# Output tiles of 128 x 2 x 512 in two buffers, and stores of 2 KB runs, in a retention and feed-forward kernel

## The chip, the cores and the metric

The kernel runs on one core of a Trainium2 chip. The metric is the device time of one execution in microseconds; the time of a kernel is the median of its runs.

## The reference

Eight batches, eight heads, 576 tokens, 64 dimensions a head: a causal retention (scores times a decay, no softmax), then a feed-forward layer with a hard swish over 4608 tokens, 512 to 2048 to 512 features. All inputs and the output are float32.

```python
scores = scale * np.matmul(q, k.transpose(0, 1, 3, 2))
ret = scores * Dmat[None, :, :, :]          # gamma ** (i - j), zero above the diagonal
x = np.matmul(ret, v) laid out as (B * S, H * D)
h = x @ w_in
g = h * np.clip(h + 3.0, 0.0, 6.0) / 6.0
out = g @ w_out
```

## The kernel before

The tokens of a batch are cut into four chunks of 128 and a tail of 64; two tails of neighbouring batches share a chunk, so there are 36 chunks. The feed-forward part works on blocks of 512 tokens: blocks 0 to 7 are the first 512 tokens of each batch, block 8 gathers the tails. Blocks are finished in the order 0, 1, 2, 3, 4, 5, 6, 8, 7.

The order of all work is written out by hand in `PROGRAM`, one word per step; each engine runs its own instructions in that order, and so does the queue of SP, which issues every load and every store. `l` loads a chunk (q, k, v, 256 KB each, in runs of 256 B), `c` casts one of the three with the decay (mostly on POOL), `x` has ACT issue a DMA transpose of q and k, `s` makes the scores on PE and masks them on DVE (tile `at`), `o` makes the retention output and the running state on PE; ACT copies the output into `xt` (L339) and, but for the last chunk of a batch, the state into `s16` (L345). The `xp` and `state` banks in PSUM have one buffer each, so the `o` of a chunk needs ACT's copies of the chunk before. `u` and `h` are the up projection: PE into a PSUM bank `ph`, then ACT (`u`, L371) and DVE (`g`, L376).

The down projection of block 0 is plain: four PSUM banks `po`, one of 128 tokens each, copied out in turn by ACT and DVE (`down_plain_end`) and stored one by one (L414). Of every other block it is a product by quadrants in the manner of Strassen: `e` builds sums of quarters of `g` on DVE (tiles `ss`), and the word `P<block>.<n>` runs one of seven products, in the order P1, P5, P6, P2, P7, P4, P3. A block of the output has four quadrants of 256 tokens by 256 features. P2 ends quadrant (0, 0), which ACT copies out (L519); P7, P4 and P3 end (1, 1), (1, 0) and (0, 1), which DVE adds up out of `accC` or `accD` and `Z` or `W` (L522, L525, L528). The four accumulators A, C, B, D and the `ph` banks share four PSUM buffers under the tag `mm`.

Each quadrant gets a tile `osb` of 128 x 2 x 256 float32 (two groups of 128 tokens), of which there are four buffers, and a store of its own right behind the word that fills it: 256 KB in runs of 1 KB (L532). For block 8 a quadrant leaves in four stores of 64 tokens, 64 KB each (`store`, L418). In `PROGRAM` other words stand between the products; block 1's stretch reads

```
P1.0 P1.1 x11 P1.2 P1.3 e1.3.0.8 s9 o8 x12 e1.4.0.8 l18 P1.4 o9 c13.0g
c13.2g c13.1g l19 s10 P1.5 P1.6 x13
```

and block 2's and 3's ends

```
P2.3 s16 c19.2g o15 c20.0g c20.1g e2.4.0.8 P2.4 s17 o16 x19 P2.5 l24 c20.2g l25 P2.6
P3.3 c23.2g s21 c24.1g o20 P3.4 l29 x23 c24.2g c25.0v c25.1g P3.5 P3.6 l30
```

where `.3` is P2, `.4` P7, `.5` P4 and `.6` P3. A tile of a tag with n buffers can be filled only when the readers of an earlier tile of that buffer are done; for `osb` that is the landing of its stores.

Of the kernel before, what the change touches and what calls it, by code (L numbers as in the profile page):

```python
# [10 lines left out]
FP32 = mybir.dt.float32  # L11
FP16 = mybir.dt.float16
ACTF = mybir.ActivationFunctionType
ALU = mybir.AluOpType
# [69 lines left out]
def kernel(  # L84
# [9 lines left out]
    nc = tc.nc  # L94
    B, H, S, D = q.shape
    NTOK, DM = out.shape
    DFF = moe_w_in.shape[1]
    P = 128
# [4 lines left out]
    NFC = DFF // P  # L103
    NCC = DM // P
    BLK = 512
    COL_UP, COL_DOWN = (5, 6, 8, 7), (4, 5, 6, 8, 7)
    gamma = [1.0 - 2.0 ** (-5.0 - h) for h in range(H)]
    lng = [float(np.log(g)) for g in gamma]
# [2 lines left out]
    work = ctx.enter_context(tc.tile_pool(name="work", bufs=2))  # L111
# [14 lines left out]
    tmat = [const.tile([P, NFC // 2, 256], FP16, name=f"tmat{i}") for i in range(4)]  # L126
    xtail = const.tile([P, NCC, BLK], FP16)
    ident = const.tile([P, P], FP16)
    zero16 = const.tile([P, BLK], FP16)
    NS16 = 2  # L130
# [170 lines left out]
    def ret2(c):  # L301
# [24 lines left out]
        if kind == 0:  # L326
            if t == 0:
                state[0] = psum.tile([P, HP, D], FP32, tag="st", name="state")
                xts[b] = work.tile([P, NCC, BLK], FP16, tag="xt", bufs=3,
                                   name="xt")  # L330
# [25 lines left out]
    def g_new(kb):  # L356
        gs[kb] = work.tile([P, NFC, BLK], FP16, tag="g", bufs=2, name="g")

    def mul(ps, lhs, rhs, start, stop, halves=True):

        if not halves:
            nc.tensor.matmul(ps, lhs, rhs, start=start, stop=stop,  # L362
                             skip_group_check=True)
            return
        for z in range(2):
            nc.tensor.matmul(ps[z * D:z * D + D], lhs[:, z * D:z * D + D], rhs,  # L366
                             start=start, stop=stop, skip_group_check=True)

    def hswish(ph, dst):
        u = work.tile([P, BLK], FP32, tag="u", bufs=3, name="u")  # L370
        nc.scalar.activation(u, ph, ACTF.Relu, bias=0.5,  # L371
                             scale=1.0 / 6.0)
        sh = list(dst.shape)
        uv = u if len(sh) == 2 else u.rearrange("p (a i) -> p a i", a=sh[1])
        pv = ph if len(sh) == 2 else ph.rearrange("p (a i) -> p a i", a=sh[1])
        nc.vector.scalar_tensor_tensor(out=dst, in0=uv, scalar=1.0,  # L376
                                       in1=pv, op0=ALU.min, op1=ALU.mult)

    def up(kb, fc, nwarm=0):
# [3 lines left out]
        xt = xts[kb] if kb < B else xtail  # L383
        ph = psum.tile([P, BLK], FP32, tag="mm", bufs=4, name="ph")
        if nwarm:
# [24 lines left out]
    def store(kb, i0, osb_ap, n0, nn):  # L410

        if kb < B:
            base = kb * S + i0
            nc.sync.dma_start(out[base:base + P, n0:n0 + nn], osb_ap)  # L414
        else:
            for z in range(2):
                base = (i0 // TAIL + z) * S + MAIN
                nc.sync.dma_start(out[base:base + TAIL, n0:n0 + nn],  # L418
                                  osb_ap[z * TAIL:(z + 1) * TAIL, :])
# [12 lines left out]

    def down_plain_end(kb, pos):
        for mc, po in enumerate(pos):
            ob = work.tile([P, DM], FP32, tag="osb", bufs=4, name="osb")
            if mc % 2:
                nc.vector.tensor_copy(ob, po)
            else:
                nc.scalar.copy(ob, po)
            store(kb, mc * P, ob, 0, DM)  # L440


    HF = NFC // 2
# [24 lines left out]
    def wq(i, j):  # L468
        return wout16[:, i * HF:(i + 1) * HF, j * 256:(j + 1) * 256]

    def product(kb, name):
        g = gs[kb]
        d = dn.setdefault(kb, {})

        def gq(i, j):
            return lambda fc, m: g[:, j * HF + fc,
                                   i * 256 + m * P:i * 256 + m * P + P]

        def sq(w):
            t_ = ssum[(kb, w)]  # L480
            return lambda fc, m: t_[:, fc, m * P:m * P + P]

        acc, first, last, lhs, rhs = {
            "P1": ("A", True, False, gq(0, 0), wq(0, 0)),
            "P2": ("A", False, True, gq(0, 1), wq(1, 0)),
            "P6": ("B", True, False, None, tmat[1]),
            "P7": ("B", False, False, None, tmat[2]),
            "P4": ("D", True, True, gq(1, 1), tmat[3]),
            "P5": ("C", True, False, None, tmat[0]),
            "P3": ("C", False, True, None, wq(1, 1)),  # L490
        }[name]
        if lhs is None:
            lhs = sq({"P6": 2, "P7": 3, "P5": 1, "P3": 4}[name])
        if first:
            d[acc] = psum.tile([P, 2, 256], FP32, tag="mm", bufs=4,
                               name="acc" + acc)
        ps = d[acc]
        for fc in range(HF):
            for m in range(2):
                mul(ps[:, m, :], lhs(fc, m), rhs[:, fc, :],  # L500
                    first and fc == 0 and m == 0, fc == HF - 1 and m == 1,
                    kb in COL_DOWN)
        if name == "P1":
            d["X"] = work.tile([P, 2, 256], FP32, tag="X", bufs=1, name="X1")
            nc.scalar.copy(d["X"], ps)
        elif name == "P6":
            d["W"] = work.tile([P, 2, 256], FP32, tag="W", bufs=1, name="W1")
            nc.vector.tensor_tensor(out=d["W"], in0=ps, in1=d["X"], op=ALU.add)
        elif name == "P5":
            return  # L510
        else:
            if name == "P7":
                d["Z"] = work.tile([P, 2, 256], FP32, tag="Z", bufs=1, name="Z1")
                nc.vector.tensor_tensor(out=d["Z"], in0=ps, in1=d["X"],
                                        op=ALU.add)
                ps = d["C"]
            ob = work.tile([P, 2, 256], FP32, tag="osb", bufs=4, name="osb")
            if name == "P2":
                nc.scalar.copy(ob, ps)  # L519
                i, j = 0, 0  # L520
            elif name == "P7":
                nc.vector.tensor_tensor(out=ob, in0=ps, in1=d["Z"], op=ALU.add)  # L522
                i, j = 1, 1
            elif name == "P4":
                nc.vector.tensor_tensor(out=ob, in0=ps, in1=d["Z"], op=ALU.add)  # L525
                i, j = 1, 0
            else:
                nc.vector.tensor_tensor(out=ob, in0=ps, in1=d["W"], op=ALU.add)  # L528
                i, j = 0, 1
            if kb < B:  # L530
                base = kb * S + i * 256
                nc.sync.dma_start(  # L532
                    out[base:base + 256, j * 256:(j + 1) * 256]
                    .rearrange("(m p) n -> p m n", p=P), ob)
            else:
                for m in range(2):
                    store(kb, i * 256 + m * P, ob[:, m, :], j * 256, 256)


    wst = {}  # L540
# [65 lines left out]
    for z in range(2):  # L606
        nc.gpsimd.iota(pos[z * TAIL:(z + 1) * TAIL, 4:5], pattern=[[0, 1]],
                       base=MAIN, channel_multiplier=1,
# [4 lines left out]
    for h in range(H):  # L613
        nc.vector.memset(lngt[:, h:h + 1], lng[h])
    nc.vector.tensor_tensor(out=etab, in1=etab, op=ALU.subtract,
                            in0=pos.unsqueeze(2).to_broadcast([P, 9, H]))
    nc.vector.tensor_tensor(out=etab, in0=etab, op=ALU.mult,
                            in1=lngt.unsqueeze(1).to_broadcast([P, 9, H]))
# [25 lines left out]
    def act(w):  # L644
# [16 lines left out]
        elif kind == "c":  # L661
            cast(order[n[0]], n[1], ENG[e])
        elif kind == "x":
            xpose(order[n[0]])
        elif kind == "y":
            xpose_pe(order[n[0]], "xp", e)
        elif kind in "sS":
            ret1(order[n[0]], *n[1:], two=(kind == "S"))
        elif kind == "o":
            ret2(order[n[0]])  # L670
        elif kind == "W":
            wload(*n)
        elif kind == "w":
            wcast(*n, e)
        elif kind == "t":
            tbuild(n[0])
        elif kind == "e":
            enc(*n)
        elif kind == "u":
            up(*n)  # L680
        elif kind == "h":
            up_half(n[0], n[1], n[2:4], *n[4:])
        elif kind == "p":
            if n[0] == 0:
                plain.extend(down_plain_begin(0))
            down_plain_part(0, plain, 2 * n[0], 2 * n[0] + 2)
            if n[0] == HF - 1:
                down_plain_end(0, plain)
        else:
            product(n[0], PROD[n[1]])  # L690
# [31 lines left out]
```

## Time and profile before

| what | value |
|---|---|
| median of 5 runs | 305.24 us (303.3 to 307.98) |
| the profiled execution | 303.3 us, its span 301.1 us |
| busy, ACT / DVE / POOL | 145.3 / 238.9 / 104.7 us |
| queue 1 (SP's loads and stores) | 120128 packets, 46.15 MB |
| queue 10 (ACT's transposes) | 29568 packets, 7.34 MB |
| stores at L532 | 28, 256 KB, 372 to 1873 ns on SP |
| stores at L418 (block 8) | 16, 64 KB, 540 to 1146 ns on SP |
| stores at L414 (block 0) | 4, 256 KB, in runs of 2 KB |
| first and last copy at L519 | 80.3 and 291.6 us |
| mean granted TensorE clock | 0.993 |

The span goes from the first to the last instruction. An engine's busy time leaves out its queue's issuing and waiting. A line of a timeline gives the start, the duration, the engine, the line of the kernel, the operation, and what it writes and reads; in square brackets stand the idle time before it and what ended that. "SPq" and "ACTq" are the engines' instruction queues, where DMAs are issued. The landing of a DMA is when its last completion has come.

### The profile page before, as it was taken

Reading aid. Unit: us, or ns where it says so; the run is one execution under the profiler, and the core shown is the slowest. Engines: PE = TensorE matmul, PEld = TensorE weight load, DVE = VectorE, ACT = ScalarE, POOL = GpSimd, SP = SyncE. Lnnn points to the kernel's source line nnn. Section 1 sums busy time; section 2 is a strip of 40 time slices with the busy share of each in tenths; the row PEclk is TensorE's granted clock in tenths of the full one; section 3 lists DMA queues with packets and bytes.
Section 4 is the critical chain, followed back from the end, with each engine's and each line's share of the span. In section 5 each row is a group of like instructions: output and inputs, shape, how many; then the busy total and the mean of one; then the engine's idle time right before and its main releaser. Section 6 shows DMA issues by size and latency. Waiting matters only on the chain.

```text
span 301.1 us, 8762 instructions
## 1 busy us (share of the span) xinstructions
PE 290.1 (96%) x3695; PEld 209.6 (70%) x3695; DVE 238.9 (79%) x341; ACT 145.3 (48%) x267; POOL 104.7 (35%) x116
## 2 busy tenths in 40 slices
PE   8889998998999999999999999999999999999994
PEld 3565354787788878547854796579657975895693
DVE  6757744989978999798778997998699768857953
ACT  2778704864237723475157424753476136306610
POOL 5354644866248636454942122334200000000000
PEclk9979999999999999999999999999999999999999
DMA  7999999999999999999999998998522130014003
GB/s 246 306 359 386 223 290 205 222 208 211 268 157 188 247 241 215 190 196 251 244 193 266 236 201 174 244 243 128 131 20 53 39 107 0 3 47 97 0 27 117
DMA packets 149735, 54.05 MB, mean 179 GB/s; under 512 B 134848, under 2 KB 145088, under 8 KB 149696
## 3 DMA queue, kind: packets, MB, share of 16 engines
q1 hardware_dynamic: 120128, 46.15, 70.2%
q10 hardware_dynamic: 29568, 7.34, 19.1%
q8 instruction: 29, 0.48, 0.7%
q14 instruction: 10, 0.08, 0.1%
HBM read 36.70 MB, written 9.44 MB: 153 GB/s over the span
## 4 chain that ended last, share of the span: by engine, by line
PE 86%; DVE 5%; ACT 3%; DMA 2%; POOL 2%; issue 1%; POOLq 0%; ACTq 0%
PE ph L362 19%; PE ph L366 18%; PE accB L366 6%; PE accC L366 6%; PE accA L366 6%; PE po L362 5%; PE accB L362 4%; PE xp L309 3%; PE sc L284 3%; PE accD L366 3%; DMA st<-in_q_dram 2%; PE accA L362 2%; PE accC L362 2%; PE xp L254 2%; DVE ss L464 2%; DVE g L376 2%
## 5 line engine op out<-in xcount | busy, mean ns | idle before, releaser
L371 ACT ACTIVATE u<-ph 128x512 f32<-128x512 f32 x144 | 84.5, 597 | 63.4 <-PE ph L362 26.9
L376 DVE SCALAR_TENSOR_TENSOR g<-u,ph 128x512 f16<-128x512 f32 x144 | 94.7, 683 | 23.2 <-ACT u L371 22.1
L362 PE MATMUL ph<-xt,win 128*128 128x256 f16 (+1 forms) x464 | 72.5, 314 | 0.0
L362 PEld LDWEIGHTS <-win 128*128 128x128 f16 x464 | 44.4, 98 | 23.2
L177 POOL TENSOR_TENSOR qk<-st,tq 128x512 f16<-128x512 f32 x29 | 32.1, 1107 | 49.7 <-PE state L334 15.6
L366 PEld LDWEIGHTS <-win 128*64 128x64 f16 x512 | 28.7, 110 | 24.4
L177 POOL TENSOR_TENSOR v<-st,tkv 128x512 f16<-128x512 f32 x29 | 32.5, 1125 | 35.7 <-DMA st<-in_v_dram 17.5
L295 DVE TENSOR_TENSOR at<-sc,mask 128x1024 f16<-128x1024 f32 (+1 forms) x34 | 39.0, 1155 | 5.8 <-PE sc L284 5.7
L366 PE MATMUL ph<-xt,win 128*64 128x512 f16 x384 | 42.8, 379 | 0.0
L366 PEld LDWEIGHTS <-ss 128*64 128x64 f16 x640 | 34.5, 110 | 0.5 <-DVE ss L464 0.3
L177 POOL TENSOR_TENSOR qk<-st,tkv 128x512 f16<-128x512 f32 x26 | 29.0, 1114 | 8.5 <-DMA st<-in_k_dram 8.4
L339 ACT ACTIVATE xt<-xp 128x512 f16<-128x512 f32 x32 | 19.1, 597 | 19.6 <-PE xp L315 17.1
L362 PEld LDWEIGHTS <-g 128*128 128x128 f16 x208 | 19.6, 98 | 10.4 <-issue 2.0
L366 PEld LDWEIGHTS <-g 128*64 128x64 f16 x480 | 26.1, 110 | 0.6
L464 DVE TENSOR_TENSOR ss<-g 128x1024 f16<-128x1024 f16 (+1 forms) x30 | 23.5, 793 | 0.3
L309 PE MATMUL xp<-at,v 128*64 128x128 f16 x288 | 20.5, 228 | 1.0 <-ACT xt L339 0.8
L362 PEld LDWEIGHTS <-ss 128*128 128x128 f16 x192 | 18.3, 98 | 3.2 <-DVE ss L464 0.9
L366 PE MATMUL accB<-tmat,ss 128*64 128x256 f16 x320 | 19.2, 273 | 0.0
L366 PE MATMUL accA<-wout,g 128*64 128x256 f16 x320 | 19.1, 273 | 0.0
L309 PEld LDWEIGHTS <-v 128*64 128x64 f16 x288 | 14.7, 111 | 6.1 <-issue 3.1
L519 ACT COPY osb<-accA 128x512 f32<-128x512 f32 x8 | 4.7, 585 | 28.1 <-PE accA L366 17.2
L345 ACT CAST s<-state 64x256 f16<-64x256 f32 x48 | 17.3, 361 | 0.5
(94 smaller groups left out, 319.1 us busy)
## 6 DMA issues: line engine op xcount, KB each, us to landing
st<-in_v_dram SPq DMA_DIRECT2D x32, 256.0 KB, 6.2
out_dram<-osb SPq DMA_DIRECT2D x32, 256.0 KB, 4.8
st<-in_q_dram SPq DMA_DIRECT2D x28, 256.0 KB, 5.7
st<-in_k_dram SPq DMA_DIRECT2D x28, 256.0 KB, 5.8
wst<-in_moe_w_in_dram SPq DMA_DIRECT2D x4, 512.0 KB, 7.4
tmat<-in_moe_w_in_dram SPq DMA_DIRECT2D x4, 512.0 KB, 8.2
wst<-in_moe_w_out_dram SPq DMA_DIRECT2D x4, 512.0 KB, 10.8
g<-in_moe_w_out_dram SPq DMA_DIRECT2D x4, 512.0 KB, 6.3
```

Of the source, the lines that this page charges most:

```text
L177: eng.tensor_tensor(out=dst, in0=st[:, ix, :, :], in1=tab.unsqueeze(2).to_broadcast([P, H, D]), op=ALU.mult)
L254: nc.tensor.matmul(ps, zero16[:, 0:P], zero16[:, 0:w], start=True, stop=True)
L284: nc.tensor.matmul(sc[z][:, p, :], qt[z * D:z * D + D, HP + p, :], qt[z * D:z * D + D, p, :], start=True, stop=True)
L295: nc.vector.tensor_tensor(out=dst, in0=src, op=ALU.mult, in1=m[:, :].unsqueeze(1).to_broadcast([P, n, P]))
L309: nc.tensor.matmul(xp[rows[z], p, :], vt[:, 2 * p + z, :], at[:, z, p, :], start=(p == 0), stop=False, skip_group_check=True)
L339: nc.scalar.activation(xts[b][:, :, t * P:(t + 1) * P], xp, ACTF.Copy, scale=0.125)
L345: nc.scalar.copy(s16[rows[z], :, rows[z]], sp[rows[z], :, :])
L362: nc.tensor.matmul(ps, lhs, rhs, start=start, stop=stop, skip_group_check=True)
L366: nc.tensor.matmul(ps[z * D:z * D + D], lhs[:, z * D:z * D + D], rhs, start=start, stop=stop, skip_group_check=True)
L371: nc.scalar.activation(u, ph, ACTF.Relu, bias=0.5, scale=1.0 / 6.0)
L376: nc.vector.scalar_tensor_tensor(out=dst, in0=uv, scalar=1.0, in1=pv, op0=ALU.min, op1=ALU.mult)
L464: nc.vector.tensor_tensor(out=dst, in0=a, in1=c, op=op)
```

## The change

The tile `osb` becomes 128 x 2 x 512 float32, twice as large, with two buffers in place of four: one tile for the upper 256 tokens of a block (quadrants (0, 0) and (0, 1)), one for the lower (1, 0) and (1, 1). The four output operations of a block write halves of these tiles. Except for block 7, which is done last, nothing is stored behind P2 and P7; behind P4 the whole lower tile is stored, and behind P3 the whole upper one, 512 KB each in runs of 2 KB. Block 7 stores each quadrant as before, out of the wider tile. Block 8 leaves in eight stores of 64 tokens x 512 features, four behind P4 and four behind P3. In block 0 the four 128-token results go in pairs into two tiles; their four stores stay as they are. `PROGRAM` is not touched.

```diff
+    LAST_BLK = 7
...
     def down_plain_end(kb, pos):
         for mc, po in enumerate(pos):
-            ob = work.tile([P, DM], FP32, tag="osb", bufs=4, name="osb")
-            if mc % 2:
-                nc.vector.tensor_copy(ob, po)
+            if mc % 2 == 0:
+                ob = work.tile([P, 2, DM], FP32, tag="osb", bufs=2, name="osb")
+                nc.scalar.copy(ob[:, 0, :], po)
             else:
-                nc.scalar.copy(ob, po)
-            store(kb, mc * P, ob, 0, DM)
+                nc.vector.tensor_copy(ob[:, 1, :], po)
+            store(kb, mc * P, ob[:, mc % 2, :], 0, DM)
...
-            ob = work.tile([P, 2, 256], FP32, tag="osb", bufs=4, name="osb")
+            i, j = {"P2": (0, 0), "P7": (1, 1), "P4": (1, 0), "P3": (0, 1)}[name]
+            if ("o", i) not in d:
+                d["o", i] = work.tile([P, 2, DM], FP32, tag="osb", bufs=2,
+                                      name="osb")
+            ob = d["o", i][:, :, j * 256:(j + 1) * 256]
             if name == "P2":
                 nc.scalar.copy(ob, ps)
-                i, j = 0, 0
...
             else:
-                nc.vector.tensor_tensor(out=ob, in0=ps, in1=d["W"], op=ALU.add)
-                i, j = 0, 1
+                nc.vector.tensor_tensor(
+                    out=ob, in0=ps, in1=d["W" if name == "P3" else "Z"],
+                    op=ALU.add)
+            if kb == LAST_BLK:
+                js = slice(j * 256, (j + 1) * 256)
+            elif name in ("P4", "P3"):
+                js = slice(0, DM)
+            else:
+                return
+            ob = d["o", i][:, :, js]
             if kb < B:
                 base = kb * S + i * 256
                 nc.sync.dma_start(
-                    out[base:base + 256, j * 256:(j + 1) * 256]
+                    out[base:base + 256, js]
                     .rearrange("(m p) n -> p m n", p=P), ob)
             else:
                 for m in range(2):
-                    store(kb, i * 256 + m * P, ob[:, m, :], j * 256, 256)
+                    store(kb, i * 256 + m * P, ob[:, m, :], 0, DM)
```

More of the change, by code (lines that the diff above doesn't have):

```diff
@@ L516, in product @@
                 ps = d["C"]
-            ob = work.tile([P, 2, 256], FP32, tag="osb", bufs=4, name="osb")
+            i, j = {"P2": (0, 0), "P7": (1, 1), "P4": (1, 0), "P3": (0, 1)}[name]
[3 more added lines that the diff above has]
+            ob = d["o", i][:, :, j * 256:(j + 1) * 256]
             if name == "P2":
                 nc.scalar.copy(ob, ps)
-                i, j = 0, 0
[L521 to L526, printed above, removed]
-            else:
-                nc.vector.tensor_tensor(out=ob, in0=ps, in1=d["W"], op=ALU.add)
-                i, j = 0, 1
+            else:
+                nc.vector.tensor_tensor(
[8 more added lines that the diff above has]
+            ob = d["o", i][:, :, js]
             if kb < B:
```

## The prediction

> **What bounds the kernel now.** First the page: who is busy, and when.
>
> ```profile
> PE 290.1 (96%) x3695; PEld 209.6 (70%) x3695; DVE 238.9 (79%) x341; ACT 145.3 (48%) x267; POOL 104.7 (35%) x116
> ...
> PE   8889998998999999999999999999999999999994
> ...
> DMA  7999999999999999999999998998522130014003
> ```
>
> PE is busy for 290.1 of 301.1 us, and the DMA engines are full until about slice 28 (210 us): the loads and stores of that stretch stand in a long queue. Next the chain of waits in order of time, around the first stores of the product blocks.
>
> ```profile
> 93.27 7.24 DMA st<-in_q_dram
> ...
> 103.92 0.61 ACT u L371
> 104.55 1.89 DVE g L376 x3
> 106.47 1.08 DVE ss L464
> 107.57 1.96 DVE ss L464
> 109.53 0.05 issue
> 109.58 1.92 PE accB L362 x16
> ```
>
> Up to 109.58 us the chain crosses a load and other engines; from there to 296.79 it stays on PE, without a pause worth naming. So whatever holds PE after 109.58 lengthens the run one for one, and little can be gained there: the list of PE's waits from 99 to 290 us has one entry, 0.2 us. Then SP's queue in order of time:
>
> ```profile
> 97.06 1.79 SPq L157 DMA_DIRECT2D st<-in_v_dram  x1
> 99.33 0.81 SPq L532 DMA_DIRECT2D out_dram<-osb  x1
> ...
> 104.74 0.90 SPq L532 DMA_DIRECT2D out_dram<-osb  x1
> 107.80 0.37 SPq L157 DMA_DIRECT2D st<-in_q_dram  x1
> ...
> 110.77 1.76 SPq L532 DMA_DIRECT2D out_dram<-osb  x2
> ```
>
> These are block 1's stores. Their tiles were written at 80.3 to 88.2 us, but the stores leave at 99.33, 104.74, 110.77 and 112.11: SP runs some 20 us behind the engines. Its last two, looked at alone:
>
> ```profile
> L532 SPq DMA_DIRECT2D out_dram<-osb x2: 416/831/1246, 110.8 to 112.1; - x2
> ...
> DMA to landing us min/median/max: 5.3/5.7/6.0
> ```
>
> They land at 110.77 + 6.0 = 116.8 and 112.11 + 5.3 = 117.4. Last, ACT and PE in block 2, whose P2 is the next to want an output tile:
>
> ```profile
> 114.40 0.58 ACT L519 COPY osb<-accA 128x512 f32<-128x512 f32 x1 [1.34 <-PE accA L362]
> 115.22 0.60 ACT L339 ACTIVATE xt<-xp 128x512 f16<-128x512 f32 x1 [0.23 <-PE xp L315]
> 115.71 0.74 ACT L345 CAST s<-state 64x256 f16<-64x256 f32 x2
> ```
>
> ```profile
> 117.41 0.25 PE L309 MATMUL xp<-at,v 128*64 128x128 f16 x2
> 117.49 0.22 PE L315 MATMUL xp<-qkT,s 128*64 128x128 f16 x2
> ```
>
> **The change, part by part.** *Fewer, wider stores.* Six blocks go from four 256 KB stores to two of 512 KB, block 8 from sixteen of 64 KB to eight of 128 KB, block 7 keeps its four: 20 issues fewer. The bytes are the same. Between 99 and 113 us the two last of block 1 land 0.6 us apart, 256 KB in 0.6 us, some 400 GB/s, and no slice in which stores run alone shows more than 389; block 0's stores, which have runs of 2 KB already, landed no closer (0.8 us). So I price the longer runs at nothing, ends 0 and 0.2 us per 512 KB. An issue on SP costs 0.37 us unobstructed (block 6); two per block is 0.75 us of SP's time, which lies beneath the DMA queue's 5 to 6 us of backlog. If that cover were gone, loads would come 0.75 us earlier, and from 109.58 on PE does not wait for loads.
>
> The Trainium skill, "DMA: Bandwidth & Descriptors", section "Anatomy of one DMA — SWDGE (gpsimd) path", gives each DMA a fixed 2.0 us for its own path, which would by estimate favour merging by 2.0 us per store on a path; here stores left by SP land 0.6 us apart, so the fixed part overlaps. The same page's "Rules for kernel authors" speaks against this change: issue a DMA early and wait for it late. The sum below needs neither.
>
> *When the stores leave.* P2's and P7's stores go; P4's carries the lower rows, P3's the upper. In SP's order block 1's three loads between P2 and P7, and three between P7 and P4, move ahead of two stores. Those loads gain one or two issues (0.8 to 1.7 us); nothing on PE waits for it. Block 2's go likewise: its last store still leaves behind two more chunk loads.
>
> *Two buffers in place of four.* The bytes of SBUF are the same, but the tile that P2 of a block fills is P2's and P3's of the block before, if buffers are taken in turn, and its store is now the **last** of that block. Before, P2 took the buffer whose store left first (99.33, landed 104.9; the copy came at 114.40, so 9.5 us to spare). The prices, block by block:
>
> Block 1 after block 0: the first two plain stores land at 78.1 and 78.9, P2's copy comes at 80.25; the other two at 81.1 and 81.8, P7's write at 83.9. Nothing, with 1.4 us as cover.
>
> Block 2 after block 1: as many bytes stand ahead of the last landing as before, so it stays at 117.4, and ACT's copy waits from 114.40 till then. Behind it on ACT stand the xt copy and the two s casts, 0.58 + 0.60 + 0.74 less 0.1 of overlap: 1.8 us. PE's next retention chunk needs both; it gets them at 117.4 + 1.8 = 119.2 in place of 117.49. **Price 1.7 us**, straight onto PE. Ends: SP sat for 2.1 us ahead of the load at 107.80, waiting for a transpose whose place in the order can shift when DMAs go; without it the landing is 115.3 and the price below nothing, so 0. Such a wait can also fall on the store itself; the longest that one of the stores shows is 2.7 us (block 0's fourth), which makes 4.4. I take the row as it stands.
>
> Block 3 after block 2: that last store leaves at 145.09 and takes 5.9, landing at 151.0; the copy comes at
>
> ```profile
> 145.77 0.59 ACT L519 COPY osb<-accA 128x512 f32<-128x512 f32 x1 [4.66 <-PE accA L362]
> 146.67 0.60 ACT L339 ACTIVATE xt<-xp 128x512 f16<-128x512 f32 x1 [0.32 <-PE xp L315]
> ...
> 153.00 0.60 ACT L371 ACTIVATE u<-ph 128x512 f32<-128x512 f32 x1 [5.73 <-PE ph L362]
> ```
>
> ACT stalls 5.2 us, 3.5 after the first delay. But ACT was going to idle 5.73 us before its next u, and PE meanwhile has P7, P4 and P3 (3 x 1.75 us) until it wants accA's PSUM bank at 151.94, now 153.6; the copy ends at 151.6. The transpose behind it leaves 5 us later for a chunk that PE takes at 164. Nothing, with 2 us as cover; ends 0 and 1.5, if the store lands 3.5 later.
>
> Block 4 after block 3: landed at 167.05 + 4.6 = 171.7, copy at 177.03: nothing. Blocks 5 to 8 and 7: SP has caught up by 207 us, stores land in 2 to 5 us, a block lies 26 us or more from the next: nothing.
>
> *Strided tile halves and the end.* A store or an engine now touches half of a tile while the other half is in use. ACT's xt copy at 58.06 and PE's ph matmul at 58.41 on other columns of the same xt tile overlapped in time, so halves do not wait for each other. The writes keep their 128x512 shape: 0.58 and 0.69 us. Block 7 stores as before, its end is unchanged.
>
> Sum: 1.7 us. The profiled execution took 303.3 with a span of 301.1 us (2.2 around it), so 305.0, span 302.8. It was the fastest of the five runs; on their median of 305.24 the forecast is 306.9, +0.6%.
>
> **Rivals.** *No stall* (25%): SP's 2.1 us wait goes, or the wider stores land sooner, and block 1's last landing falls before 115.7, the point from which PE is not delayed. For it: the wait is a transpose's, not the data's. Against it: the queue is backlogged either way. 305.2, not slower; 304.8 with the 0.2 us and the gaps on PE filled.
> *A later landing* (18%): a wait for a transpose lands ahead of the store, or block 3's cover breaks as well: 2.6 to 4.4 us, 307.8 to 309.6. For it: six such waits stand on SP, 8.8 us in all, and a stalled ACT issues its transposes later.
> *The other buffer* (10%): P2 takes the buffer freed first. Its copy then waits for 116.1 or so (0.4 us), and in block 3 P7's write, at 149.37 before, waits for 151.0; P3's matmuls need accC read by it and start at 151.7, not 150.19, less the shift: 1.1. Together 1.5: 306.7.
> *Faster* (5%): earlier loads shorten the chain. It crosses a load only at 93.27, before the first store that moves. 303.5.
> *The change not as told*: seven blocks' 1024 data packets of 1 KB must be halved, so queue 1 must show at least 3584 packets fewer than 120128, or it did something else.
>
> **How the numbers follow.** The forecast (0.8 to 2.6 us, 306.0 to 307.8) gets 42%. Half a per cent, about what a measurement can tell from no change, is 1.5 us. Slower: two thirds of the forecast (28%), the later landing (18%), 4% of the other buffer: 50%. Same: 14 + 21 + 6 = 41%. Faster: 5 + 4 of no stall: 9%. The range runs from 304.6, no stall with little noise, to 309.4.
>
> **What would show it.** The stores of whole blocks down from 28 to 16 issues and the tail block's from 16 to 8; in block 2 ACT's osb copy ended by a DMA out_dram<-osb, some 3 us long, and an idle PE of 1 to 2 us before L309 or L315; in block 3 a stall of 3 to 5 us on ACT with PE unmoved. PE idle anywhere else, or no wait at either copy, would make the steps wrong.

## The result, and the profile after

| kernel | median | runs | ratio to before, 95% |
|---|---|---|---|
| before | 305.13 us (302.12 to 308.06) | 85 | |
| changed | 306.58 us (303.52 to 309.97) | 43 | 1.005 [1.0033, 1.0066] |

The change costs about 1.5 us: half a per cent. That is just at what a measurement can tell from no change, but the interval lies above 1, so it isn't zero. (Ratios leave disturbed runs out, so they can differ a little from the quotient of two medians.) The profiled execution of the changed kernel took 305.75 us, its span 304.0.

The page's lines on busy time, on SP's queue and on the stores of whole blocks (count, size, median us from issue to landing):

```profile
PE 289.5 (95%) x3695; PEld 208.8 (69%) x3695; DVE 240.3 (79%) x341; ACT 145.3 (48%) x267; POOL 103.9 (34%) x116
...
q1 hardware_dynamic: 116224, 46.15, 70.2%
...
out_dram<-osb SPq DMA_DIRECT2D x12, 512.0 KB, 5.9
```

The change does what it says: the same 46.15 MB in 3904 packets fewer, twelve stores of 512 KB (and four of 256 KB in block 7), at the same work of PE. SP's queue in order of time, around the stores of blocks 1 and 2:

```profile
109.25 1.06 SPq L158 DMA_DIRECT2D st<-in_v_dram  x1
110.42 2.53 SPq L538 DMA_DIRECT2D out_dram<-osb  x2
113.04 0.85 SPq L158 DMA_DIRECT2D st<-in_q_dram  x1
...
135.46 0.57 SPq L538 DMA_DIRECT2D out_dram<-osb  x1
...
144.82 1.68 SPq L158 DMA_DIRECT2D st<-in_v_dram  x1
146.61 1.19 SPq L538 DMA_DIRECT2D out_dram<-osb  x1
```

Block 1's stores now leave together, at 110.42 and 112.55 (the second start is from the single records of the pair), and land at 117.04 and 119.81. Block 2's second store leaves 11 us behind its first, at 146.61, since six loads stand between the two words, and lands at 152.23. Who waits for these landings is told by ACT and DVE in order of time:

```profile
117.10 0.58 ACT L524 COPY osb<-accA 128x512 f32<-128x512 f32 x1 [1.91 <-DMA out_dram<-osb]
117.58 0.60 ACT L340 ACTIVATE xt<-xp 128x512 f16<-128x512 f32 x1
118.07 0.75 ACT L346 CAST s<-state 64x256 f16<-64x256 f32 x2
```

```profile
150.77 0.69 DVE L515 TENSOR_TENSOR Z<-accB,X 128x512 f32<-128x512 f32 x1 [0.55 <-PE accB L363]
152.32 0.69 DVE L526 TENSOR_TENSOR osb<-accC,Z 128x512 f32<-128x512 f32 x1 [0.85 <-DMA out_dram<-osb]
```

```profile
150.57 1.91 PE L363 MATMUL accD<-tmat,g 128*128 128x256 f16 x16
153.07 1.91 PE L363 MATMUL accC<-wout,ss 128*128 128x256 f16 x16 [0.58 <-DVE osb L526]
```

In block 2 P2's copy starts right after the **first** landing of block 1 (117.04), not the last; in `a0` below it does the same, 0.07 us behind a first landing at 118.56. Of the 1.91 us that ACT idled, 1.25 are there without any wait for a store too (`d1` below, where PE ends them), so the store's own share is 0.66 us. ACT is done with the casts at 118.82, and PE comes for them at 119.54: no wait. In block 3 it is not P2's copy but **P7's write** that waits, for the landing at 152.23, and through it PE, because P3's matmuls go into the bank that this write reads. PE's list of waits from 99 to 300 us has this one entry:

```profile
PE accC L363 <- DVE osb L526: 0.6, 1, 0.6
```

Before, no wait stands at either step, on DVE or on PE:

```profile
149.37 0.69 DVE L522 TENSOR_TENSOR osb<-accC,Z 128x512 f32<-128x512 f32 x1
...
150.19 1.91 PE L362 MATMUL accC<-wout,ss 128*128 128x256 f16 x16
```

So the two buffers are not taken in turn: what these waits show is that the next tile gets the buffer that is released first. In a block the upper tile is begun first but stored last. Block 2's upper tile sits where block 1's lower one was, and block 3's lower tile, filled by P7, gets the buffer that block 2's late store holds.

### The profile page after: what moved, and what is told of

Read it like the earlier page. It is cut to its first block, busy times and chain, and to the rows that moved or that the text cites. A ratio compares the mean times of both kernels' runs of the same rounds, so it can differ in the third digit from the quotient of the medians.

```text
span 304.0 us, 8719 instructions
## 1 busy us (share of the span) xinstructions
PE 289.5 (95%) x3695; PEld 208.8 (69%) x3695; DVE 240.3 (79%) x341; ACT 145.3 (48%) x267; POOL 103.9 (34%) x116
## 3 DMA queue, kind: packets, MB, share of 16 engines
q1 hardware_dynamic: 116224, 46.15, 70.2%
## 4 chain that ended last, share of the span: by engine, by line
PE 64%; DMA 15%; SPq 9%; DVE 4%; POOL 4%; issue 1%; ACT 1%; POOLq 0%; ACTq 0%; DVEq 0%
PE ph L367 18%; PE ph L363 12%; PE accB L367 6%; PE accA L367 6%; DMA st<-in_v_dram 5%; PE accC L367 5%; PE po L363 4%; SPq L561 4%; SPq L158 4%; DMA tmat<-in_moe_w_in_dram 3%; DMA out_dram<-osb 3%; PE accD L367 2%; PE xp L310 2%; PE sc L285 2%; DMA qkT<-qk 2%; DMA st<-in_k_dram 2%
## 5 line engine op out<-in xcount | busy, mean ns | idle before, releaser
L178 POOL TENSOR_TENSOR qk<-st,tq 128x512 f16<-128x512 f32 x29 | 30.9, 1066 | 52.7 <-DMA st<-in_q_dram 18.2
L178 POOL TENSOR_TENSOR v<-st,tkv 128x512 f16<-128x512 f32 x29 | 33.7, 1165 | 36.7 <-DMA st<-in_v_dram 10.0
```

The source lines that it names most:

```text
L178: eng.tensor_tensor(out=dst, in0=st[:, ix, :, :], in1=tab.unsqueeze(2).to_broadcast([P, H, D]), op=ALU.mult)
```

## The experiments

One length of the trace separates the kernels better than the whole time: from PE's first matmul of the product ahead of block 2's P2, into `accB` (109.58 us before), to the first matmul of P3 in block 3 (150.19 before). In these traces it holds the only waits that the two buffers made on PE. In the table: when PE gets to the first of the two, the length between them, the length from there to PE's last matmul, and the timed ratio. All lengths are differences of start times in the trace.

| kernel | reaches block 2 | to block 3's P3 | to the last matmul | timed ratio |
|---|---|---|---|---|
| before | 109.6 | 40.61 | 146.28 | |
| `b0` before, again | 111.8 | 40.60 | 146.28 | 1.0035 [1.0001, 1.0068] |
| `b1` before, third | 110.0 | 40.60 | 146.28 | one run |
| `d0` before, fourth | 112.0 | 40.61 | 146.82 | 1.0012 [0.9981, 1.0044] |
| changed | 111.7 | 41.35 | 146.28 | 1.005 [1.0033, 1.0066] |
| `a0` changed, again | 113.4 | 41.14 | 147.77 | 1.0076 [1.0039, 1.0112] |
| `d1` changed, third | 112.7 | 40.94 | 146.28 | 1.0103 [1.0064, 1.0143] |
| `d3` one buffer per half | 112.9 | 40.94 | 146.27 | 1.0058 [1.0027, 1.009] |
| `a1` three buffers | 112.1 | 40.61 | 147.08 | 1.0046 [1.0013, 1.008] |
| `a2` store ahead of loads | 111.1 | 40.61 | 146.89 | 1.0014 [0.9983, 1.0045] |
| `c3` both of these | 111.4 | 40.61 | 146.83 | 1.0006 [0.9972, 1.004] |
| `d2` both, again | 112.4 | 40.61 | 146.28 | 1.0013 [0.9978, 1.0049] |
| `c1` wide tiles, old stores | 113.0 | 40.60 | 146.28 | 1.0022 [0.9988, 1.0056] |
| `a3` store behind a third load | 112.4 | 47.38 | 149.32 | 1.0269 [1.0222, 1.0315] |

**Equal kernels.** No edit: the changed kernel twice more, the one before three times more, to see how far one execution stands for its kernel.

> The changed kernel once more, unedited, for a second profile. Theory 'buffer': its loss is one stall, in block 3, where P7's write on DVE waits for block 2's last store and PE's P3 waits for that write (0.6 us in the first profile); it shows here again, 0.3 to 2.5 us, ratio 1.003 to 1.007. Theory 'early': the 2.1 us that the first profile was late before 105 us, ahead of any store that moved, belong to the change too; then this profile is again about 2 us late there. Rival 'spread': the early 2.1 us are one execution's luck and come out anywhere from -1.5 to +2 us.

> The changed kernel, unedited, on the same chip as its cure: 'buffer' theory 1.004 to 1.009, and P7's write in block 3 again waits for a store; PE's stall there 0.3 to 2 us.

> The kernel before, unedited, for a second profile of it. In the five profiles of the changed kernel and its variants PE begins block 1's first product at 74.1 to 75.4 us, against 72.8 in the one profile of before, and block 0's fourth store leaves at 80.7 to 82.9, against 78.3. Rival 'spread': that one profile was a lucky execution; this one shows 74 to 75.5 and about 81. Theory 'early': the change makes it, and this one shows 72.3 to 73.3 and about 78. Ratio 0.998 to 1.002 either way.

> The same once more, a third profile: 'spread' 73.5 to 75.5 us for block 1's first product, 'early' 72.3 to 73.3.

> The kernel before, submitted like the others, for a second look at what no change at all measures here (1.0035 the first time). 'Chance': 0.998 to 1.002. 'Place' (a submitted kernel reads a little slower than the runs that it is set against): 1.002 to 1.005 again, and the others are to be read from there.

The loss repeats: 307.22 and 306.86 us beside 304.97 and 304.89 for the kernel before in the same groups. So does the noise: against itself the kernel before came out at 1.0035, more than expected, and at 1.0012, as 'chance' had it, in 12 runs each, and PE reached block 2 anywhere from 109.6 to 112.0 us in four executions of it. The prediction's profile was the earliest of the four. Where a later execution loses its time is seen in `b0`, PE's waits in order of time:

```profile
73.24 1.91 PE L362 MATMUL accA<-wout,g 128*128 128x256 f16 x16 [1.68 <-DVE g L376]
98.64 1.91 PE L362 MATMUL ph<-xt,win 128*128 128x256 f16 x16 [1.44 <-ACT xt L339]
101.01 0.41 PE L309 MATMUL xp<-at,v 128*64 128x128 f16 x8 [0.46 <-DVE at L295]
```

None of these has to do with an output tile. On theory 'early' the traces are less clear than on the buffer. Block 1's first product began at 73.24, 73.63 and 74.55 us in the three further executions of the kernel before, so the first of them lies within what 'early' named and the other two within 'spread'. In the ten executions with wide tiles, whatever their stores, it began at 73.9 to 75.4. The ranges overlap, but most of the wide kernels are later, and that stays unexplained. The timed ratios of `c1`, `c3` and `d2`, whose profiles are just as late, show no cost of it. The stall in block 3 also varies: 0.58 us of PE's wait in the first execution of the changed kernel, 0.38 in `a0`, none in `d1`, where 0.3 to 2 us were expected, but the late store happened to land at 151.74 and PE came later. What `d1` and `d3` have above 40.61 comes at another wait, of PE on DVE's `ss` near 145.6 (0.17 us in the list, 0.33 in PE's starts behind it); and `a0` loses 1.5 us more behind the length, of which PE's list names 0.7 on DVE's `g` and 0.4 on a transpose.

**More of the suspected wait.** One load more stands ahead of block 2's last store:

```diff
-c19.2g ... P2.5 l24 c20.2g l25 P2.6
+c19.2g ... P2.5 l24 c20.2g l25 l26 P2.6
...
-u3.4 u3.12 e3.1.0.4 c21.1g c22.2g c22.0g l26 u3.5 l27 c22.1g l28 u3.13 x21
+u3.4 u3.12 e3.1.0.4 c21.1g c22.2g c22.0g u3.5 l27 c22.1g l28 u3.13 x21
```

> The changed kernel with one more chunk load (l26) ahead of block 2's last store: the suspected wait made longer by some 3.5 to 4.5 us and nothing else. Theory 'buffer': PE's stall in block 3 grows from 0.6 to 4 or 5 us, ratio 1.014 to 1.020. Theory 'early': no change, 1.004 to 1.006.

313.15 us, +2.7%, more than expected. The store leaves at 151.68 and lands at 158.96; DVE and PE in order of time:

```profile
159.06 0.69 DVE L526 TENSOR_TENSOR osb<-accC,Z 128x512 f32<-128x512 f32 x1 [6.89 <-DMA out_dram<-osb]
```

```profile
159.80 3.57 PE L363 MATMUL accC<-wout,ss 128*128 128x256 f16 x16 [6.62 <-DVE osb L526]
```

The same two instructions wait, and for the same store: landing 6.7 us later than in the changed kernel, it holds PE 6.0 us longer. That is the proof of the place. The stall is longer than the 4 or 5 us expected, because the store left 5.1 us later than in the changed kernel and took 7.3 us to land. The rest of the excess is in the 3.57 us, where sixteen such matmuls took 1.91 before. A table by stretches of 2 us of the same execution (window, length, busy time and count of PE, PEld, DVE, ACT and POOL, then the granted clock, the DMA share and GB/s):

```profile
154.00:156.00 2.00, 0.00 (x0) 0.00 (x0) 0.00 (x0) 0.00 (x0) 0.00 (x0) 0.88 1.28 262
156.00:158.00 2.00, 0.00 (x0) 0.00 (x0) 0.00 (x0) 0.00 (x0) 1.27 (x2) 0.50 1.16 314
158.00:160.00 2.00, 0.20 (x2) 0.14 (x2) 0.94 (x2) 0.00 (x0) 0.77 (x1) 0.50 1.30 254
160.00:162.00 2.00, 2.00 (x11) 1.44 (x10) 0.95 (x2) 0.00 (x0) 0.00 (x0) 0.50 1.37 217
162.00:164.00 2.00, 2.00 (x9) 1.09 (x8) 0.59 (x1) 0.00 (x0) 0.00 (x0) 0.50 1.37 217
164.00:166.00 2.00, 2.00 (x7) 0.73 (x5) 0.36 (x2) 0.60 (x1) 0.00 (x0) 0.56 1.38 218
166.00:168.00 2.00, 2.00 (x31) 1.11 (x30) 1.43 (x3) 1.51 (x4) 0.77 (x1) 1.00 1.37 218
```

PE's clock falls to half some 2 us into the pause and stays there until about 166: six microseconds of matmuls at half speed behind a pause of 6.6. The 24 matmuls from P3's first on take 6.48 us (159.80 to 166.28) in place of 3.57 before, 2.9 more.

**The wait taken away.** A third buffer (`a1`), the store ahead of two loads (`a2`), and both (`c3`, `d2`):

```diff
-                ob = work.tile([P, 2, DM], FP32, tag="osb", bufs=2, name="osb")
+                ob = work.tile([P, 2, DM], FP32, tag="osb", bufs=3, name="osb")
...
-                d["o", i] = work.tile([P, 2, DM], FP32, tag="osb", bufs=2,
+                d["o", i] = work.tile([P, 2, DM], FP32, tag="osb", bufs=3,
```

```diff
-c19.2g ... P2.5 l24 c20.2g l25 P2.6
+c19.2g ... P2.5 c20.2g P2.6 l24 l25
```

> The changed kernel with three wide buffers in place of two. Theory 'buffer': no write of an output tile waits for a store, ratio to the kernel before 0.998 to 1.002. Theory 'early', or a cost of the merged stores themselves: 1.004 to 1.006 as with two buffers.

> The changed kernel with two buffers; in block 2 the two chunk loads l24 and l25 stand behind the last store, not ahead of it. Theory 'buffer': the store leaves some 10 us earlier, block 3's stall is gone, ratio 0.998 to 1.002; block 2's copy may still wait for block 1's store without holding PE. Theory 'early': 1.004 to 1.006. If the loads' delay by one store matters, slower than 1.006.

> Three wide buffers, merged stores, and block 2's last store ahead of l24 and l25: both cures at once, and a second measurement of merged stores without a wait for a buffer. Theory 'buffer': 0.998 to 1.002, no output write waits for a store. Rival 'merged stores': 1.003 to 1.006.

> Three wide buffers, merged stores, block 2's last store ahead of two loads, a second time: 'buffer' theory the same as the kernel before submitted alike, within 0.3%, and 1 to 2 us under the changed kernel. 'Merged stores cost something': midway or above.

In all four the length is back at 40.60 or 40.61 us. In `a2`, with two buffers, both stores of block 2 leave in one go, and P7's write has no wait; SP, then DVE:

```profile
135.24 1.08 SPq L538 DMA_DIRECT2D out_dram<-osb  x2
136.42 1.52 SPq L158 DMA_DIRECT2D st<-in_q_dram  x1
```

```profile
150.88 0.69 DVE L526 TENSOR_TENSOR osb<-accC,Z 128x512 f32<-128x512 f32 x1
```

The loads that follow the store now start 0.3 us later (136.13 in the changed kernel), and PE lists no wait for them. The times, though, follow less cleanly. `a2`, `c3` and `d2` lie at 1.0006 to 1.0014, no different from the kernel before against itself. `a1` came out at 1.0046, where none of its output tiles waits any more. That is a miss: an interval from 1.0013 to 1.008 leaves out no change, but tells it neither from the changed kernel nor from `b0`'s 1.0035. A trace does show `a1` losing 0.4 us elsewhere (PE on DVE's `g` at 194 us); the same entry is in `a2` and in `c3`, so it doesn't set `a1` apart.

**The stores alone.** The wide tile stays, in three buffers, but every quadrant is stored as before, 256 KB in runs of 1 KB:

```diff
-            if kb == LAST_BLK:
+            if True:
...
-                    store(kb, i * 256 + m * P, ob[:, m, :], 0, DM)
+                    store(kb, i * 256 + m * P, ob[:, m, :], j * 256, 256)
```

> Three wide buffers, but each quadrant stored by itself right behind its product, in 1 KB runs, block 8's too: the tiles' layout without the merged and later stores. Theory 'buffer': as with three buffers and merged stores, 0.998 to 1.003. Rival 'merged stores' (they cost something of their own, by their place or size): this one is 0.998 to 1.002 while three buffers with merged stores stays at 1.004 or more.

Queue 1 is back at 120128 packets, and the time is 305.47 us, 1.0022, beside 305.29 for `c3` with merged stores. Half as many stores of twice the run are worth nothing that can be measured here. One reading stays open: `c1` differs from `c3` in the place of block 2's last store too, and the kernel that differs from it in the merging alone is `a1`, at 1.0046. By the words of the expectation that pair speaks for the rival 'merged stores'; the two intervals overlap, and `c3` and `d2`, merged as well, lie at 1.0006 and 1.0013.

**The forecast's own premise.** Each half of a block gets a buffer of its own, so P2's copy must wait for the upper tile's store of the block before, the last one:

```diff
-                ob = work.tile([P, 2, DM], FP32, tag="osb", bufs=2, name="osb")
+                ob = work.tile([P, 2, DM], FP32, tag=f"osb{mc // 2}", bufs=1,
+                               name="osb")
...
-                d["o", i] = work.tile([P, 2, DM], FP32, tag="osb", bufs=2,
+                d["o", i] = work.tile([P, 2, DM], FP32, tag=f"osb{i}", bufs=1,
```

> The changed kernel with one wide buffer kept for the upper and one for the lower half of every block, as the forecast took it to be: P2's copy must wait for the last store of the block before. The forecast's price: in block 2 ACT waits some 3 to 5 us and PE 1.7 us (0.5 to 3); in block 3 ACT waits 3 to 5 us and PE nothing; ratio 1.004 to 1.010. If ACT's stall in block 2 is hidden from PE, 0.998 to 1.003.

306.54 us, 1.0058. ACT in blocks 2 and 3, in order of time:

```profile
118.17 0.59 ACT L525 COPY osb<-accA 128x512 f32<-128x512 f32 x1 [1.80 <-DMA out_dram<-osb]
118.65 0.60 ACT L340 ACTIVATE xt<-xp 128x512 f16<-128x512 f32 x1
119.14 0.75 ACT L346 CAST s<-state 64x256 f16<-64x256 f32 x2
...
152.87 0.58 ACT L525 COPY osb<-accA 128x512 f32<-128x512 f32 x1 [8.45 <-DMA out_dram<-osb]
```

The copies wait exactly where the prediction put them, behind the landings at 118.09 and 152.80, the first for only 0.55 of its 1.80 us of idling (1.25 without a store). Yet PE lists no wait for either: from 99 to 330 us it has 1.3 us for `xt` and 0.5 for `at` around 100 us, before these copies, and 0.2 for `ss`. In block 2 the casts end at 119.89, and PE, 3.3 us later than in the prediction's profile, comes for them at 120.72. In block 3 ACT idles 3.5 us more than `d1`'s 5.00, and PE has its three products meanwhile. The timed loss of `d3` therefore is not in a stall that this one execution shows.

## Why the prediction was right, and where it was not

The time was right: 306.9 us forecast, 306.58 measured, +0.5% where +0.6% stood, with half the chance on slower by more than half a per cent. The mechanism was only half right, and that the number fits is in part luck: the 1.7 us were put at P2's copy in block 2, where PE never waited, and the stall that came in block 3 belongs to a rival whose number, 306.7, stood 0.2 us away. The time could not tell the two apart.

- *Fewer, wider stores at nothing, ends 0 and 0.2 us.* Held. `c1` and `c3` differ by 0.2 us in 12 runs each, with `a1` as the open end named above. In `c3` block 2's two stores land at 142.79 and 144.01: 512 KB in 1.2 us, twice the 0.6 us for 256 KB.
- *Stores leave later, loads earlier, and nothing on PE.* The order is as told. That the loads gain nothing is left to `a2`, whose loads go behind the store again: 1.0014.
- *Two buffers, "if buffers are taken in turn".* **This step failed.** Buffers go by release. In the kernel before, the tiles are begun and released in one order, so its trace could not tell one rule from the other; in the changed kernel the upper tile is begun first and released last. This was the rival "the other buffer", at 10%: P2's copy waited 0.66 us for the first store and cost PE nothing, where it priced 0.4 on PE, and P7's write in block 3 waited, as it said, with 0.58 us on PE where it priced 1.1. A PE idle at another place than L309 or L315 was also what the prediction named as showing its steps wrong.
- *Block 2's price of 1.7 us.* It did not arise in the changed kernel, whose copy waits for the other store. As a sum it holds better than `d3`'s profile suggests. A price of this kind is the difference of two positions of one execution: the landing of block 1's last store plus 1.8 us, and PE's arrival, 7.9 us behind its entry to block 2 (117.49 less 109.58; in `d3` the same). `d3` is an execution with an early landing: 118.09 + 1.8 stands against 112.90 + 7.9, so 0.9 us to spare. The same estimate from the changed kernel's row, 119.81 + 1.8 against 111.71 + 7.9, gives 2.0 us; over the profiles with merged stores (`a3` aside) it gives 1.6 to 2.0 in five, 0.9 in `d2`, and nothing in `d1` and `d3`. So `d3`'s timed 1.0058, some 1.7 us, may well be this stall in executions that were not profiled; its one trace does not show it.
- *Block 3: ACT's stall is hidden.* Held in `d3`: 3.5 us on ACT, none on PE.
- *Block 1 after block 0: 1.4 us of cover.* Broken once: in `a0` P7's write waited 0.8 us for block 0's fourth store, landed at 86.76. PE was not held.
- *Blocks 4 to 8, 7, and the end.* Held: no output tile holds PE there. Past block 3's P3 the changed kernel's PE takes 146.28 us, as before, in two of three executions; of `a0`'s 1.5 us more PE's list puts 1.1 on other waits.

What stays **open** is the rest of the size. The stall seen on PE is 0.58, 0.38 and 0 us in three executions, 0.3 on average, against about 1.5 us by the runs. Three executions are few for a difference of two positions, and another trace shows that it can be larger. `a1` issues its stores in the same order, only with a third buffer. There block 2's late store landed at 154.07, and P3 started at 152.71. Where P3 waited, it started 0.84 us behind that landing (`after`, `a0`, `a3`), so by estimate two buffers would have held PE 154.07 + 0.84 - 152.71 = 2.2 us in that execution. A stall from 0 to 2.2 us can hold the 1.5, but four executions don't give its mean. The other candidate is the stretch up to block 2, where PE arrives at 109.6 to 112.0 us in the kernel before and at 111.1 to 113.4 in all the wide ones. Whether the wide tiles shift that was not tried apart; `c1`, `c3` and `d2`, which arrive at 111.4 to 113.0 and do not wait, time like the kernel before. That curing the wait also cures the time is likely from `a2`, `c3` and `d2`, not certain beside `a1`.

No version beat the kernel before; the best, merged stores with three buffers and the store ahead of the loads, equals it.

## What to carry to other kernels

Before merging stores, ask when the merged source is released: a store that waits for its last half holds the first half's buffer too, and in one queue it may stand behind loads that the halves would have passed. A stall's price is the distance between a transfer's landing and an engine's arrival; take both from the same execution, and from several executions, since here the arrival alone moved by 2.4 us and the landing moved too. And a trace in which buffers are filled and released in the same order says nothing of how they will be handed out when the orders part.

## What the runs showed of the hardware

A pause of PE costs more than itself once it is long enough. With 0.58 us the granted clock stayed at 1.00 in the changed kernel; with 6.6 us it fell to 0.50 and cost 2.9 us more on the matmuls behind. The Trainium skill, "TensorE: Matmul & The Clock Gate", section "Part 1: The HAM clock gate", has the gate watch windows of about 3.4 us, halve the clock after an idle one and restore it after a busy one. By the 0.88 and the 0.56 of two rows of `a3`, the clock fell at about 155.5 us, 2.3 us into the pause, and rose at about 165.8, 6 us after work had resumed. The 10.2 us between are three windows of the page's length, which agrees; but the fall came after less than one whole window of idleness, and the rise after more than one of work, so 3.4 us is not how long a pause must be.

The device time exceeds the span by 1.79 us on average in the changed kernel and by 1.72 to 1.79 in the others that hold two wide tiles (`a0`, `a2`, `a3`, `d1`, `d3`), but by 2.15 to 2.20 in the kernel before and in all that hold three (`a1`, `c1`, `c3`, `d2`), each an average over the runs of a group. These 0.4 us lie outside the profiled span, and nothing here explains them. They hide part of the loss: by spans the changed kernel is 2 us longer (median 304.7 to 302.7), by time 1.5. So it is with `a2`: its median span is 304.05 us beside 302.8 for the kernel before in its group, 0.4% longer.
